# Attention with a local window and a three-way max MLP: the second transpose of each head takes 64 or 96 keys instead of 128

## The chip, the cores and the metric

The kernel runs on one core of a Trainium2 chip. The metric is the device time of one launch in microseconds; a lower time is better. The median of three runs of the kernel before is 864.78 us (864.51 to 865.18).

## The reference

Eight batches of eight heads. Each head has 512 local and 32 global positions of 64 numbers. A local query sees the 32 global keys and the local keys at most 32 positions away; a global query sees all 544 keys. The 8 x 544 = 4352 rows of 512 numbers then go through the MLP.

```python
s_g = scale * np.matmul(q_g, k_all.transpose(0, 1, 3, 2))
out_g = np.matmul(sm(s_g), v_all)
...
mask = np.abs(pos[:, None] - pos[None, :]) <= window      # window = 32
s_ll = np.where(mask, s_ll, -1000000000.0)
s_l = np.concatenate([s_lg, s_ll], axis=-1)
out_l = np.matmul(sm(s_l), np.concatenate([v_g, v_l], axis=2))
...
h = np.maximum(np.maximum(x @ w1, x @ w2), x @ w3)
return h @ w_out
```

## The kernel before, in words

**Tiles of attention.** A pair of heads p has four tiles t of 128 local queries; there are 8 x 4 pairs and so 128 tiles `sl = 4 p + t`, each for both heads j of its pair. `WIN` gives the window of keys of each t, global keys included: 192 keys for t = 0 and 3, and 224 for t = 1 and 2. Each tile passes these steps:

- `scores` (L296): q times k for each head into a bank S. VectorE adds the mask and finds the extreme (L324), ScalarE takes the exponential (L326), and the row is divided by its sum (L329 to L331). The result lies with a query in each partition and the window's keys along the row. For the first 16 tiles (`EARLY`) it stays in `early`, an F32 buffer of four places with rows of 256. For the other 112 a DMA (L333) writes it into one of two buffers `prob` with rows of 256 (type F32R).
- `trans` (L337): turns the probabilities so that keys lie in partitions. The row of 256 is two blocks c of 128 keys. For each head j and block c, a transpose on TensorE (L345) takes the block as its stationary operand and an identity of 128 columns as the moving one (`one` for the early tiles, `identr` for the others), and writes 128 x 128 numbers into a quarter of the bank T. The pool `psT` holds one such bank (`bufs=1`). A copy, and from tile 20 on a subtraction for the low part, takes all 512 columns of T to `pt`.
- `transg` (L356): the same for the global queries' rows, `probg`, into a bank S (L363).
- `pv` (L373): v times the turned probabilities into the bank O. The first 20 tiles use 64 rows of output for each head (L383); the others 128 rows (L391). The rows of v that stand against the keys 192 to 255, or 224 to 255, of a block are zeros.

Since all 256 columns of a row are turned but only 192 or 224 are written, the rest of `early` and `prob` is set to zero once: `early` by L120, and `prob`, with `probg` and `qgz`, by `clear` (L130). Both run on GpSimd (POOL).

**The MLP.** `layer1` (L412) and `layer2` (L438) are generators that issue one matmul at a time (L423, L444). The main loop (L547) is a hand-written order: for each tile it calls the attention steps of the current tile and the ones ahead, and `fill(n)` takes n matmuls of the MLP of the batch before in between, so that TensorE has work while the other engines do softmax. Inside a tile the order is: `trans` of the next tile, 4 MLP matmuls, scores of a later tile, 4, `pv`, global scores, 3, `transg`, 7 (somewhat more in the first 32 tiles). At the end `late` does four pairs' remaining global rows with outputs of 64 rows (L269, L499) and transposes at L489, and the global rows pass the MLP last.

**Order and balance.** `least` deals copies and subtractions to VectorE, ScalarE and GpSimd by a running account of their loads. The framework orders the instructions of the first tiles by its own rules; further on the order of the calls stands.

Of the kernel before, what the change touches and what calls it, by code (L numbers as in the profile page):

```python
# [9 lines left out]
F32 = mybir.dt.float32  # L10
# [20 lines left out]
WIN = [(0, 192), (96, 224), (256, 224), (384, 192)]  # L31
# [19 lines left out]
def f32(ap):  # L51
    return ap.bitcast(F32)


def body(ctx, tc, kin, qin, vin, min_, win, out):
    nc = tc.nc
    act, dve, pool, pe = nc.scalar, nc.vector, nc.gpsimd, nc.tensor
# [7 lines left out]
    psT = ctx.enter_context(tc.tile_pool(name="psT", bufs=1, space=PSUM))  # L65
# [26 lines left out]
    def sub(out, a, b, psum=False):  # L92
        n = width(out)
        c = {"d": n * 1.04 + (160 if psum else 110)}
        if not psum:
            c["p"] = n * 2.32 + 130
        (dve if least(c) == "d" else pool).tensor_tensor(out=out, in0=a, in1=b, op=ALU.subtract)  # L97

    def copy(out, a, psum=False):
        n = width(out)  # L100
        c = {"d": n * (1.04 if psum else 0.52) + (160 if psum else 150), "a": n * 0.833 + (150 if psum else 190)}
        if least(c) == "d":
            dve.tensor_copy(out=out, in_=a)
        else:
            act.copy(out=out, in_=a)  # L105
# [11 lines left out]
    one = const.tile([128, 128], F32, name="one")  # L117
    make_identity(nc, one)
    early = const.tile([128, 4, 2, 256], F32, name="early")
    pool.memset(early[:, :, :, 192:256], 0.0)  # L120
    identr = const.tile([128, 128], F32R, name="identr")
    dve.tensor_copy(out=identr, in_=one)
    mask = const.tile([128, 2, 224], F32, name="mask")
# [2 lines left out]
    prob = [const.tile([128, 2, 256], F32R, name=f"prob{i}") for i in range(2)]  # L126
    probg = [const.tile([128, 3, 128], F32R, name=f"probg{i}") for i in range(2)]
    qgz = const.tile([128, 2, 160], F32R, name="qgz")

    def clear():  # L130
        for t in (*prob, *probg, qgz):
            pool.memset(f32(t), 0.0)

    raw, wt = {}, {}
# [2 lines left out]
        return wt[n][:, 512 * a:512 * a + 512]  # L137

    xg = const.tile([128, NP, B, SG], F32, name="xg")

    spare = [moe.tile([128, 2, 512], I32, name="spare", tag=f"h{f}") for f in (4, 5)]
    loaded, marks = [0], {}
# [194 lines left out]
    def trans(sl):  # L337
        if sl >= NS:
            return
        s = sc.pop(sl)  # L340
        ps = psT.tile([128, 512], F32, name="T")
        pr, ident = (ps, one) if sl < EARLY else (ps.bitcast(F32R), identr)
        for j in range(2):
            for c in range(2):
                pe.transpose(pr[:, 256 * j + 128 * c:256 * j + 128 * c + 128], s[:, j, 128 * c:128 * c + 128], ident)  # L345
        src = ps.rearrange("p (x q) -> p x q", q=128)
        if sl < NAT:
            pt = pts[sl] = att.tile([128, 2, 2, 160], F32, name="pt", tag="pt")
            copy(pt.rearrange("p j c q -> p (j c) q")[:, :, 0:128], src, True)
        else:  # L350
            pt = pts[sl] = att.tile([128, 2, 2, 2, 160], F32R, name="pt", tag="pt")
            v = pt.rearrange("p j c a q -> p (j c) a q")
            copy(v[:, :, 0, 0:128], src, True)
            sub(v[:, :, 1, 0:128], src, f32(v)[:, :, 0, 0:128], True)
# [189 lines left out]
    load_v(SEQ[3], 3)  # L544
    load_weight()
    trans(SEQ[0])
    for i, sl in enumerate(SEQ):  # L547
        p, t = divmod(sl, 4)
        b = p // NP
        settle(4500)  # L550
        if i % 16 == 0 and b > 1:
            fill(400)
            mm[0] = moe_local(b - 1)
        trans(tile_at(i + 1))
        first = i < 32
        fill(6 if first else 4)
        next_scores(i + 3)
        if i < 16:
            if i == 7:
                clear()  # L560
            if i in (10, 12):
                load_k((i - 2) // 2)
            if i == 14:
                split_k(5)
                load_k(6)
        elif t == 3:
            split_k(p + 2)
            load_k(p + 3)
# [95 lines left out]
```

## Time and profile before

| | |
|---|---|
| median of the runs | 864.78 us (864.51 to 865.18) |
| the profiled execution | 865.03 us |
| its span, first to last instruction | 862.9 us |
| mean granted TensorE clock | 0.984 |
| busy: PE, PEld, DVE, ACT, POOL | 820.8, 692.3, 632.0, 505.9, 528.8 us |

PE is TensorE's matmuls and transposes and PEld its weight loads, which run beside them; DVE is VectorE, ACT ScalarE, POOL GpSimd and SP the queue that issues DMAs. A row of a group reads: line, engine, operation, output<-inputs, the part of the array (rows*columns), sizes, count | busy us, mean ns of one | idle time of the engine before them and who ended it. A row of the timeline reads: start in us, length in us, engine, line, operation, output<-inputs, array part, sizes, count of instructions merged. The recorded ends of matmuls are modelled, and matmuls overlap, so a matmul's step is read from one start to the next and not from its length.

### The profile page before, as it was taken

The numbers are of one execution on the slowest core, as the hardware profiler recorded it, in microseconds if no ns is written. First come the engines' busy times: TensorE is split into PE (matmuls) and PEld (weight loads), VectorE is DVE, ScalarE is ACT, GpSimd is POOL, SyncE is SP. The second block draws the span as 40 slices with busy tenths as digits, with TensorE's granted clock in tenths as the row PEclk, the third lists the DMA queues.
The fourth block names the chain that finished last, engine by engine and source line by source line (L and its number), as shares of the span: only waits on it lengthen the run. The fifth ranks groups of instructions, "written<-read, shape, count | busy, mean of one in ns | idle before, by whom it ended". The sixth has DMA issues, their size and how long they took to land.

```text
span 862.9 us, 16816 instructions
## 1 busy us (share of the span) xinstructions
PE 820.8 (95%) x4736; PEld 692.3 (80%) x4736; DVE 632.0 (73%) x2181; ACT 505.9 (59%) x1430; POOL 528.8 (61%) x698
## 2 busy tenths in 40 slices
PE   6878788999999999999999999999999999999997
PEld 5566678988888888888888888888888888777796
DVE  6999798977788888878787888778887876322111
ACT  5666566766676666666666666676666666212111
POOL 5778887866677667756776667667676656111211
PEclk9999688999999999999999999999999999999999
DMA  9743533353334333443325333433344333221000
GB/s 317 261 162 119 160 120 106 111 160 104 111 106 133 120 94 105 130 132 94 101 90 160 106 111 106 136 114 93 109 133 134 94 90 99 77 72 29 28 25 25
DMA packets 99580, 98.72 MB, mean 114 GB/s; under 512 B 21152, under 2 KB 87968, under 8 KB 99488
## 3 DMA queue, kind: packets, MB, share of 16 engines
q1 hardware_dynamic: 99344, 97.43, 36.4%
q8 instruction: 38, 0.62, 0.3%
q14 instruction: 54, 0.44, 0.2%
q10 hardware_dynamic: 144, 0.23, 0.1%
HBM read 60.39 MB, written 8.91 MB: 80 GB/s over the span
## 4 chain that ended last, share of the span: by engine, by line
PE 80%; DVE 8%; POOL 4%; issue 2%; DMA 2%; ACT 2%; SPq 1%; POOLq 0%; DVEq 0%; ACTq 0%
PE pm L423 46%; PE pm L444 15%; PE O L391 6%; PE S L321 5%; PE T L345 4%; PE S L273 1%; POOL h L97 1%; DMA raw<-w_in 1%; POOL w L97 1%; DVE spare L164 1%; DVE spare L160 1%; POOL early L115 1%; PE S L363 1%; DVE s L324 1%; POOL xs L97 1%
## 5 line engine op out<-in xcount | busy, mean ns | idle before, releaser
L423 PE MATMUL pm<-xs,w 128*128 128x512 f32 (+1 forms) x2160 | 504.3, 372 | 5.8 <-POOL w L97 4.5
L423 PEld LDWEIGHTS pm<-xs,w 128*128 128x128 f32 x2160 | 351.9, 193 | 56.4 <-POOL w L97 5.1
L444 PE MATMUL pm<-w,h 128*128 128x512 f32 x612 | 160.4, 399 | 1.7 <-POOL h L97 1.7
L97 POOL TENSOR_TENSOR qs<-qraw,qs 128x256 fp32r<-128x256 f32 x108 | 83.3, 771 | 79.2 <-issue 44.9
L97 POOL TENSOR_TENSOR h<-m,h 128x512 fp32r<-128x512 f32 (+1 forms) x60 | 72.0, 1199 | 88.8 <-ACT h L105 88.8
L444 PEld LDWEIGHTS pm<-w,h 128*128 128x128 f32 x612 | 107.2, 188 | 22.3 <-POOL h L97 3.4
L115 POOL TENSOR_SCALAR s<-s,z 128x224 f32<-128x224 f32 (+1 forms) x212 | 97.0, 466 | 42.3 <-ACT lox L105 19.2
L326 ACT ACTIVATE s<-s,nm 128x192 f32<-128x192 f32 (+1 forms) x224 | 103.3, 462 | 25.0 <-DVE nm L324 16.5
L432 DVE TENSOR_TENSOR m<-pm,m 128x512 f32<-128x512 f32 (+1 forms) x120 | 72.9, 607 | 49.2 <-PE pm L423 47.7
L97 DVE TENSOR_TENSOR pt<-T,pt 128x512 fp32r<-128x512 f32 x108 | 74.5, 690 | 40.7 <-ACT pt L105 38.4
L324 DVE CUSTOM_DVE_ANT_0 s<-S,mask 128x192 f32<-128x192 f32 (+1 forms) x224 | 74.8, 370 | 14.2 <-PE S L321 7.5
L97 POOL TENSOR_TENSOR vs<-vraw,vs 128x256 fp32r<-128x256 f32 x107 | 80.8, 755 | 5.3 <-ACT vs L105 4.1
L105 ACT CAST pt<-T 128x512 fp32r<-128x512 f32 x89 | 52.2, 586 | 48.6 <-PE T L345 48.5
L391 PE MATMUL O<-pt,vs 128*128 128x320 f32 (+1 forms) x432 | 78.3, 303 | 0.1
L391 PEld LDWEIGHTS O<-pt,vs 128*128 128x128 f32 x432 | 70.6, 190 | 9.1 <-DVE pt L97 0.3
L97 POOL TENSOR_TENSOR kst<-kraw,kst 64x576 fp32r<-64x576 f32 x48 | 70.4, 1467 | 5.4 <-DVE nm L324 1.7
L321 PEld LDWEIGHTS S<-kst,qs 128*128 128x128 f32 x432 | 64.9, 194 | 9.7 <-DVE nmg L277 1.8
L105 ACT CAST qs<-qraw 128x256 fp32r<-128x256 f32 x90 | 36.6, 406 | 58.9 <-PE S L321 37.6
L399 DVE TENSOR_TENSOR xr<-O,lox 64x160 f32<-64x160 f32 x216 | 67.9, 314 | 2.8
L345 PEld LDWEIGHTS T<-identr,prob 128*128 128x128 f32 x448 | 50.7, 142 | 19.9 <-ACT s L326 4.7
L321 PE MATMUL S<-kst,qs 128*128 128x192 f32 (+1 forms) x432 | 66.2, 275 | 0.1
L397 DVE TENSOR_TENSOR lox<-O,lox 64x320 f32<-64x320 f32 x108 | 51.6, 478 | 13.5 <-ACT lox L105 7.2
(115 smaller groups left out, 1139.2 us busy)
## 6 DMA issues: line engine op xcount, KB each, us to landing
vraw<-v_in SPq DMA_DIRECT2D x132, 128.0 KB, 2.3
qraw<-q_in SPq DMA_DIRECT2D x108, 128.0 KB, 2.2
prob<-s SPq DMA_DIRECT2D x56, 224.0 KB, 2.4
raw<-w_in SPq DMA_DIRECT2D x24, 512.0 KB, 4.8
prob<-s SPq DMA_DIRECT2D x56, 192.0 KB, 2.3
kraw<-k_in SPq DMA_DIRECT2D x27, 320.0 KB, 3.1
out_dram<-o SPq DMA_DIRECT2D x32, 256.0 KB, 2.3
qn<-q_in SPq DMA_DIRECT2D x21, 128.0 KB, 3.5
```

Of the source, the lines that this page charges most:

```text
L97: (dve if least(c) == "d" else pool).tensor_tensor(out=out, in0=a, in1=b, op=ALU.subtract)
L105: act.copy(out=out, in_=a)
L115: pool.tensor_scalar(out=out, in0=a, scalar1=col, scalar2=1.0, op0=ALU.mult, op1=ALU.mult)
L321: pe.matmul(ph[j][:, 0:n], lhsT=qs[sl][:, a, 128 * j:128 * j + 128], rhs=kst[p][:, j, c0:c0 + n], start=(a == 0), stop=(a == 1))
L324: dve.tensor_tensor_reduce(out=s[:, j, 0:n], in0=ph[j][:, 0:n], in1=mask[:, (1, 0, 1, 0)[t], 32 * (t == 0):32 * (t == 0) + n], scale=-0.12 ...
L326: act.activation(out=s[:, j, 0:n], in_=s[:, j, 0:n], func=AF.Exp, bias=nm[:, j:j + 1], scale=-1.0, accum_out=z[:, j:j + 1])
L345: pe.transpose(pr[:, 256 * j + 128 * c:256 * j + 128 * c + 128], s[:, j, 128 * c:128 * c + 128], ident)
L391: pe.matmul(o[:, j, 0:320].rearrange("p (a q) -> p a q", a=2)[:, :, 0:n], lhsT=vs[sl][:, 2 * j + c].rearrange("p a d -> p (a d)"), rhs=pt[ ...
L399: dve.tensor_tensor(out=xr[p][64 * j:64 * j + 64, t], in0=o[0:64, j, 0:160], in1=lo[:, j], op=ALU.add)
L423: pe.matmul(ps[:, 0:n], lhsT=weight(3 * f + i, w)[:, 128 * k:128 * k + 128], rhs=xs[k][:, a, c0:c0 + n], start=(q == 0), stop=(q == 11))
L432: dve.tensor_tensor(out=m[:, 0:n], in0=ps[:, 0:n], in1=m[:, 0:n], op=ALU.max)
L444: pe.matmul(ps, lhsT=hh[f][:, a, 128 * t:128 * t + 128], rhs=weight(18 + f, w), start=(q == 0), stop=(q == 17))
```

## The change

The second transpose of each head takes only the window's valid keys as its stationary block: `n = WIN[sl % 4][1] - 128`, so 64 keys for t = 0 and 3 and 96 for t = 1 and 2. It writes n rows of its quarter of T. T is no longer taken from its pool for each tile: it is one fixed bank, `turned`, which VectorE sets to zero once at the start, so that the rows that are not written hold finite numbers when the copy takes all 512 columns. The clears of `early` and of the two `prob` go; those of `probg` and `qgz` stay.

```diff
     early = const.tile([128, 4, 2, 256], F32, name="early")
-    pool.memset(early[:, :, :, 192:256], 0.0)
...
     def clear():
-        for t in (*prob, *probg, qgz):
+        for t in (*probg, qgz):
             pool.memset(f32(t), 0.0)
...
+    turned = psT.tile([128, 512], F32, name="T")
+    dve.memset(turned, 0.0)
...
         s = sc.pop(sl)
-        ps = psT.tile([128, 512], F32, name="T")
+        ps, n = turned, WIN[sl % 4][1] - 128
         pr, ident = (ps, one) if sl < EARLY else (ps.bitcast(F32R), identr)
         for j in range(2):
-            for c in range(2):
-                pe.transpose(pr[:, 256 * j + 128 * c:256 * j + 128 * c + 128], s[:, j, 128 * c:128 * c + 128], ident)
+            pe.transpose(pr[:, 256 * j:256 * j + 128], s[:, j, 0:128], ident)
+            pe.transpose(pr[0:n, 256 * j + 128:256 * j + 256], s[:, j, 128:128 + n], ident)
```

PE's order around the transposes of a tile with a window of 192 keys, in the stretch where the MLP's matmuls stand between the steps; `pm` is the MLP's bank, and the sizes are the output's rows x columns. Before:

```order
L363 MATMUL S<-identr,probg_96 128x128
L423 MATMUL pm<-xs,w_400 128x512 x7
L345 MATMUL T<-identr,prob_95 128x128 x4
L423 MATMUL pm<-xs,w_442 128x512 x4
L321 MATMUL S<-kst,qs 128x224 x4
```

After:

```order
L364 MATMUL S<-identr,probg_95 128x128
L424 MATMUL pm<-xs,w_395 128x512 x7
L345 MATMUL T<-identr,prob_94 128x128
L346 MATMUL T<-identr,prob_94 64x128
L345 MATMUL T<-identr,prob_94 128x128
L346 MATMUL T<-identr,prob_94 64x128
L424 MATMUL pm<-xs,w_436 128x512 x4
L322 MATMUL S<-kst,qs 128x224 x4
```

The four transposes stand in the same place. The first and third are as before; the second and fourth have outputs of 64 rows, and in tiles with a window of 224 keys outputs of 96.

POOL's order at the start of the program, where it makes the identity (`masks.py`), clears buffers and divides the first tiles' rows (L115). Before:

```order
masks.py:197 MEMSET one 128x128
L120 MEMSET early 128x8x64
masks.py:199 ISA
masks.py:199 AFFINE_SELECT one<-one 128x128
L132 MEMSET prob_94 128x512
L115 TENSOR_SCALAR early<-early,z 128x224
L132 MEMSET prob_95 128x512
L115 TENSOR_SCALAR early<-early,z 128x224
L132 MEMSET probg_96 128x384
L132 MEMSET probg_97 128x384
L132 MEMSET qgz 128x320
L115 TENSOR_SCALAR early<-early,z 128x192 x2
```

After:

```order
masks.py:197 MEMSET one 128x128
L131 MEMSET probg_95 128x384
masks.py:199 ISA
masks.py:199 AFFINE_SELECT one<-one 128x128
L131 MEMSET probg_96 128x384
L115 TENSOR_SCALAR early<-early,z 128x224 x2
L131 MEMSET qgz 128x320
L115 TENSOR_SCALAR early<-early,z 128x192 x2
```

Three clears are gone, and the clears of `probg` have moved to the places of two of them.

## The prediction

> **What bounds the kernel now.** I read the page first, then the table of stages, then PE's waits, and last the timeline of PE around the edited instructions.
>
> ```profile
> PE 820.8 (95%) x4736; PEld 692.3 (80%) x4736; DVE 632.0 (73%) x2181; ACT 505.9 (59%) x1430; POOL 528.8 (61%) x698
> PE 80%; DVE 8%; POOL 4%; issue 2%; DMA 2%; ACT 2%; SPq 1%; POOLq 0%; DVEq 0%; ACTq 0%
> ```
>
> PE is busy for 95% of the span and makes up 80% of the chain that ended last. The profiled execution took 865.03 us, 862.9 of them span; the median of the runs is 864.78, so 0.25 comes off at the end. Shares are averages, so the table of stages is next (stretch, length, PE busy, PEld, DVE, ACT, POOL, granted clock, DMA share, GB/s):
>
> ```profile
> 80.00:110.00 30.00, 21.56 (x140) 19.24 (x139) 25.05 (x73) 16.38 (x45) 25.74 (x26) 0.77 0.47 147
> 110.00:300.00 190.00, 182.22 (x1088) 159.27 (x1087) 160.39 (x563) 127.93 (x370) 135.13 (x184) 0.96 0.39 118
> 300.00:500.00 200.00, 199.31 (x1101) 168.20 (x1100) 164.11 (x581) 133.47 (x382) 136.36 (x186) 1.00 0.37 112
> 500.00:735.00 235.00, 234.00 (x1291) 197.49 (x1290) 184.34 (x670) 154.30 (x438) 155.04 (x213) 1.00 0.37 111
> ```
>
> From 110 to 735 us PE has hardly a hole, while DVE, the next, has 16 to 22% free. Who PE waits for in that stretch (total, times, longest):
>
> ```profile
> PE S L363 <- DMA probg<-sg: 5.1, 2, 3.0
> PE pm L444 <- POOL h L97: 1.7, 4, 0.7
> PE S L363 <- DVE nm L324: 1.5, 1, 1.5
> PE T L345 <- DMA prob<-s: 0.7, 1, 0.7
> PE T L345 <- DVE z L330: 0.2, 1, 0.2
> ```
>
> That is 9.2 us in 625. So what the edit adds to or takes from PE's own time there reaches the end almost whole. Where the edited transposes lie:
>
> ```profile
> L345 PE MATMUL T<-identr,prob 128*128 128x128 f32 x448 | 52.5, 241 | 5.8 <-DMA prob<-s 5.5 <-DVE z L330 0.2
> L345 PEld LDWEIGHTS T<-identr,prob 128*128 128x128 f32 x448 | 50.7, 142 | 19.9 <-ACT s L326 4.7 <-ACT xr L105 0.8 <-issue 0.7
> L345 PE MATMUL T<-one,early 128*128 128x128 f32 x64 | 12.9, 291 | 12.0 <-POOL early L115 11.5 <-ACT early L113 0.3
> L383 PEld LDWEIGHTS O<-pt,vraw 128*64 128x64 f32 x112 | 7.1, 141 | 3.2 <-issue 1.7 <-ACT pt L105 0.3 <-DMA qn<-q_in 0.2
> ```
>
> ```profile
> L345 PE MATMUL T<-identr,prob x432: 220/245/328, 111.6 to 734.1; 128*128 128x128 f32 x144
> ```
>
> 448 is four for each of 112 tiles; 432 of them, 108 tiles, start between 111.6 and 734.1 us, so inside the full stretch. Windows of 192 keys leave 64 for the second block and those of 224 leave 96; each is every second tile. So **54 tiles with 64-key blocks and 54 with 96-key blocks** lie where PE is the bound.
>
> **The change, part by part: the 64-key blocks.** The pair "128*128" in these rows is the part of the array that an instruction takes. PV of the early tiles (L383) shows that an output of 64 rows runs as "128*64". The program built from the changed kernel says the same of the new transposes: 128x64 for 64 keys, 128x128 for 96. So in each 64-key tile PE goes 128-128, 128-64, 128-128, 128-64 and back: four changes of width where there were none. What that costs is read from starts, since ends are modelled. First, today's group:
>
> ```profile
> 402.03 1.09 PE L423 MATMUL pm<-xs,w 128*128 128x512 f32 x4
> 402.96 0.45 PE L345 MATMUL T<-identr,prob 128*128 128x128 f32 x4
> 403.25 0.70 PE L423 MATMUL pm<-xs,w 128*128 128x512 f32 x2
> ...
> 403.55 0.62 PE L423 MATMUL pm<-xs,w 128*128 128x512 f32 x2
> ```
>
> Four 512-column matmuls take 402.96 − 402.03 = 0.93, so 0.23 each. Four transposes take 0.29, and the matmul behind them 403.55 − 403.25 = 0.30: from the first transpose to the second matmul, 0.59. The ordinary step of one such transpose, alone among wide matmuls, and then the steps with changes of width around them:
>
> ```profile
> 401.22 0.22 PE L363 MATMUL S<-identr,probg 128*128 128x128 f32 x1
> 401.28 1.84 PE L423 MATMUL pm<-xs,w 128*128 128x512 f32 x7
> ```
>
> ```profile
> 769.65 0.40 PE L423 MATMUL pm<-xs,w 128*128 128x512 f32 x1
> 769.97 0.31 PE L499 MATMUL O<-gt,vn 128*64 128x32 f32 x4
> 770.11 0.40 PE L499 MATMUL O<-gt,vraw 128*64 128x32 f32 x6
> 770.44 0.28 PE L489 MATMUL S<-identr,probg 128*128 128x128 f32 x1
> 770.65 0.42 PE L499 MATMUL O<-gt,vraw 128*64 128x32 f32 x6
> ```
>
> ```profile
> 31.51 0.44 PE L345 MATMUL T<-one,early 128*128 128x128 f32 x2
> 31.87 0.43 PE L383 MATMUL O<-pt,vraw 128*64 128x128 f32 x2
> 32.24 0.85 PE L423 MATMUL pm<-xs,w 128*128 128x256 f32 x5
> ```
>
> ```profile
> 747.11 0.74 PE L423 MATMUL pm<-xs,w 128*128 128x512 f32 x2
> ...
> 747.45 0.40 PE L423 MATMUL pm<-xs,w 128*128 128x512 f32 x1
> ```
>
> The ordinary step is 0.06. A 512-column matmul before narrow ones takes 0.32, which is 0.09 over its 0.23: the array empties before the other width may start. The transpose between two narrow groups, 770.44 to 770.65, is the same instruction on the same identity as ours, and takes 0.21: 0.15 over its 0.06, of which 0.09 is again the emptying and 0.06 its own weight load, which nothing covers after a change. The two directions cost alike: a wide pair at 31.51 takes 0.36 and a narrow pair 0.37. And the first 512-column matmul after narrow work takes 0.34 to the next.
>
> So the new group is 0.06 + 0.09 = 0.15 for the first transpose (its load is still ahead of time), 0.21 for each of the other three, and 0.34 for the matmul behind them: 1.12. Net 1.12 − 0.59 = 0.53 us a tile. 54 × 0.53 = **+28.6 us**. This is the term that decides.
>
> The two 64-key tiles of the 112 that come before 111.6 us lie where PE is busy 21.56 of 30 us: between 0 and 2 × 0.53 = 1.1; I take +0.3. Some of the 9.2 us of waits in the full stretch can shrink when PE comes later: between 0 and −2; I take −0.5.
>
> [...]
>
> **The 96-key blocks.** They keep the wide array, so no change of width. Their loads are a quarter shorter at best. Loads cost today's group 0.59 − 4 × 0.06 − 0.23 = 0.12 beyond its streaming, and two of four blocks shrink: between 0 and −0.06 a tile; I take −0.02, since the recorded load is 142 ns for 128 columns and 141 for 64, which shows no gain at all: 54 × −0.02 = **−1.1** (0 to −3.2). That 96 rows cost a change too is a rival below.
>
> **The early tiles.** Eight of 16 have 64 keys. Their PV is narrow already, so the step from the last transpose to PV loses its change of width: 0 to 2 changes more a tile, at 0.15, is 0 to 2.4 us, in a stage where PE waits for others. Against it stand the clears that POOL loses:
>
> ```profile
> L132 POOL MEMSET prob<- 128x512 f32 x2 | 1.1, 526 | 0.0
> ...
> L120 POOL MEMSET early<- 128x512 f32 x1 | 0.5, 529 | 0.0
> ...
> PE T L345 <- POOL early L115: 11.5, 12, 1.6
> ...
> 7.69 0.39 DVE early L324
> ```
>
> They are 1.6 us ahead of POOL's first multiplications, for which PE waits: 0 to −1.6. I put the two together at **0** (−1.6 to +2.4). The new clear of T on DVE stands before DVE's first step of the chain at 7.69, where DVE waits for scores: nothing, or 0.7 (a 128x512 pass) without that cover. The fixed bank adds no wait: T had one buffer before, and its transposes already waited for the copies out of it. Behind its first 80 instructions PE's order is the same; among those some score matmuls trade places, which I price at nothing.
>
> Sum: 28.6 + 0.3 − 0.5 − 1.1 + 0 = 27.3; 865.03 + 27.3 = 892.3, less 0.25: **892 us**. With the small bounds of each term, 886 to 897.
>
> **The rivals.**
>
> *Narrower loads pay (faster).* The mechanism is the load of the block. If a group of transposes in one bank changes width without emptying the array, half of the 0.12 goes in 64-key tiles (0.06) and a quarter in 96-key ones (0.03): 54 × 0.09 = 4.9, so 860. It decides if a change costs under 0.02. For it: loads follow each other closely in the group. Against it: each change of width in these rows, between five kinds of instruction, shows a price. Chance 0.05. [...]
>
> *Half price.* The next load goes out while the array empties, and only the 0.09 is left: 4 × 0.09, less the 0.12 of load delay that is there today, is 0.24 a tile, 13 us: 878. Against it stands the 0.21. Chance 0.07.
>
> *Transposes slow down when narrow.* At the pace of the early ones, (0.36 − 0.15)/2 = 0.105 instead of 0.06, 112 narrow transposes cost 5 more: 897. At four times the 0.06 it is 20 more: 912. No narrow transpose is in this trace. Chance 0.10, the most of it at the lower end. [...] Against the fourfold price, two plain products of 160 columns of the same type took 0.19:
>
> ```profile
> 406.24 0.35 PE L273 MATMUL S<-kst,qgz 128*128 128x160 f32 x2
> 406.43 0.89 PE L423 MATMUL pm<-xs,w 128*128 128x512 f32 x3
> ```
>
> *96 rows change the width too.* Another 54 × 0.53: 920. No 96-row output is in the trace. Chance 0.03.
>
> *Nothing happens.* The chip runs 64 columns as wide; then only the clears are left: 864. Chance 0.02.
>
> **How the numbers follow.** The forecast keeps 0.73. It is 886 to 897; for 8 in 10 I reach up to 902 for the slower narrow transposes and down to 880 towards half price. About 0.2% (1.7 us) is what a measurement of this kernel can tell from none. Faster: the first rival, 0.05, and half of the last, 0.06 in all. Same: 0.01 for the rest of the last, and 0.01 for a price that just cancels, 0.02. Slower: 0.92.
>
> **What would show it.** In the profile after, the narrow transposes should stand as "128*64", 128 of them, and the 96-key ones on the wide array. From the first transpose to the second matmul behind it a 64-key group should take about 1.1 us, a 96-key one 0.55 to 0.6. PE's busy share should stay near 95%, and the span grow between 110 and 765 us alone. I am wrong if the group stays near 0.6, if a 96-key group grows too, or if PE's waits change by more than a few us.

## The result and the profile after

| | before | after |
|---|---|---|
| median, us | 864.78 | 859.88 (859.73 to 860.80, 4 runs) |
| the profiled execution, us | 865.03 | 859.92 |
| its span, us | 862.9 | 858.0 |
| ratio to before | | 0.9945, 95% interval 0.9933 to 0.9957 |

The changed kernel is 4.9 us faster, 0.55%. The forecast was 892, in a range of 880 to 902: the direction was wrong.

The page after, its totals and the chain by engine:

```profile
PE 813.2 (95%) x4736; PEld 683.5 (80%) x4736; DVE 631.0 (74%) x2182; ACT 505.8 (59%) x1430; POOL 526.4 (61%) x695
PE 82%; DVE 5%; DMA 5%; POOL 4%; issue 2%; ACT 1%; SPq 0%; DVEq 0%; POOLq 0%; ACTq 0%
```

PE bounds the kernel as before, with 7.6 us less of busy time. The stages, in the columns of the table in the prediction:

```profile
80.00:110.00 30.00, 20.27 (x133) 17.86 (x133) 25.50 (x76) 16.83 (x49) 25.85 (x26) 0.83 0.45 144
110.00:300.00 190.00, 180.08 (x1091) 156.45 (x1092) 159.77 (x565) 129.08 (x372) 134.28 (x184) 0.98 0.39 119
300.00:500.00 200.00, 199.27 (x1109) 167.72 (x1108) 165.03 (x582) 133.91 (x384) 137.37 (x189) 1.00 0.37 113
500.00:735.00 235.00, 233.96 (x1297) 197.24 (x1297) 183.52 (x662) 152.81 (x433) 153.23 (x209) 1.00 0.36 110
```

PE is nearly as full as it was, but each stretch from 110 us on holds more instructions (300 to 500 us: 1109 for 1101). The granted clock differs from the kernel before up to 300 us (0.83 for 0.77 and 0.98 for 0.96), so the two traces are compared behind 150 us as well, where it is 1.00 in both. The transposes of the full stretch, weight loads and matmuls (least, median and longest ns; first and last start):

```profile
L345 PEld LDWEIGHTS T<-identr,prob x216: 137/141/182, 110.2 to 728.7; 128*128 128x128 f32 x108
L345 PE MATMUL T<-identr,prob x216: 220/225/329, 110.3 to 728.8; 128*128 128x128 f32 x108
L346 PEld LDWEIGHTS T<-identr,prob x216: 109/118/155, 110.3 to 728.8; 128*64 128x64 f32 x54, 128*96 128x96 f32 x54
L346 PE MATMUL T<-identr,prob x216: 221/225/308, 110.4 to 728.8; 128*64 128x128 f32 x54, 128*96 128x128 f32 x54
```

The same transposes ran from 111.6 to 734.1 us before and run from 110.3 to 728.8 now: 622.5 us have become 618.5. So 4.0 us are gained in the full stretch and 1.3 ahead of it, of which 0.4 goes again behind it (128.8 from the last to the end before, 129.2 now). Behind 150 us, at the same granted clock, the gain is almost the same: from the eleventh later tile to the last transpose it is 734.1 − 150.1 = 584.0 us before and 728.8 − 148.7 = 580.1 now, so the clock is not what made the stretch shorter. The narrow blocks stand as "128*64" and "128*96", and their loads are shorter: a median of 118 ns over both for 141, and by width a median of 110 for 64 columns and 125 for 96.

One 64-key group:

```profile
406.08 0.22 PE L345 MATMUL T<-identr,prob 128*128 128x128 f32 x1
406.14 0.23 PE L346 MATMUL T<-identr,prob 128*64 128x128 f32 x1
406.21 0.22 PE L345 MATMUL T<-identr,prob 128*128 128x128 f32 x1
406.27 0.22 PE L346 MATMUL T<-identr,prob 128*64 128x128 f32 x1
406.33 0.69 PE L424 MATMUL pm<-xs,w 128*128 128x512 f32 x2
...
406.63 0.40 PE L424 MATMUL pm<-xs,w 128*128 128x512 f32 x1
```

The steps are 0.06, 0.07, 0.06 and 0.06, where the forecast had 0.15 and three times 0.21. The weight loads of the same group:

```profile
405.85 0.14 PEld L345 LDWEIGHTS T<-identr,prob 128*128 128x128 f32 x1
406.09 0.11 PEld L346 LDWEIGHTS T<-identr,prob 128*64 128x64 f32 x1
406.15 0.14 PEld L345 LDWEIGHTS T<-identr,prob 128*128 128x128 f32 x1
406.23 0.11 PEld L346 LDWEIGHTS T<-identr,prob 128*64 128x64 f32 x1
406.29 0.53 PEld L424 LDWEIGHTS pm<-xs,w 128*128 128x128 f32 x3
```

The next load starts 0.08 after one of 128 columns (406.15 to 406.23) and 0.06 after one of 64 (406.23 to 406.29), and the transpose or matmul that needs it starts 0.04 behind its load (406.27, 406.33). From the first transpose to the second matmul it is 406.63 − 406.08 = 0.55 us, where the forecast had 1.12 and the kernel before 0.59. For all groups behind 111 us that a 512-column matmul follows, the medians of this length in us, worked out from the starts in the traces, are the measure of the experiments below. In the kernel before and in the one with 128-column products, whose groups are all alike, the median is over both kinds.

| kernel | 64-key groups (49) | 96-key groups (49) |
|---|---|---|
| before | 0.598 | 0.598 |
| after | 0.540 | 0.566 |
| narrow blocks as plain F32R products | 0.563 | 0.616 |
| 128-column blocks as plain F32R products | 0.674 | 0.674 |
| narrow blocks as plain F32 products | 1.418 | 0.838 |
| only 64-key tiles narrow | 0.540 | 0.599 |
| only 96-key tiles narrow | 0.598 | 0.563 |
| both wide blocks first | 0.536 | 0.568 |
| all second blocks 32 columns | 0.528 | 0.528 |

### The profile page after: what moved, and what is told of

It is laid out like the page before. It is cut to its first block, busy times and chain, and to the rows that moved or that the text cites. A ratio compares the mean times of both kernels' runs of the same rounds, so it can differ in the third digit from the quotient of the medians.

```text
span 858.0 us, 16764 instructions
## 1 busy us (share of the span) xinstructions
PE 813.2 (95%) x4736; PEld 683.5 (80%) x4736; DVE 631.0 (74%) x2182; ACT 505.8 (59%) x1430; POOL 526.4 (61%) x695
## 4 chain that ended last, share of the span: by engine, by line
PE 82%; DVE 5%; DMA 5%; POOL 4%; issue 2%; ACT 1%; SPq 0%; DVEq 0%; POOLq 0%; ACTq 0%
PE pm L424 47%; PE pm L445 16%; PE O L392 7%; PE S L322 5%; PE T L345 2%; DMA raw<-w_in 2%; PE T L346 2%; PE S L274 1%; POOL h L97 1%; DMA qn<-q_in 1%; POOL xs L97 1%; PE S L364 1%; POOL w L97 1%; POOL early L115 1%; DMA vraw<-v_in 1%
## 5 line engine op out<-in xcount | busy, mean ns | idle before, releaser
L115 POOL TENSOR_SCALAR s<-s,z 128x224 f32<-128x224 f32 (+1 forms) x212 | 97.0, 467 | 42.8 <-ACT lox L105 18.5
L105 ACT CAST h<-m 128x512 fp32r<-128x512 f32 (+1 forms) x59 | 32.9, 558 | 40.6 <-DVE m L433 40.5
```

What stands on the lines that cost most here:

```text
L115: pool.tensor_scalar(out=out, in0=a, scalar1=col, scalar2=1.0, op0=ALU.mult, op1=ALU.mult)
```

## The experiments

Theory A kept as much of the prediction as the result allows: the price of a change of width is real for plain products (an ordinary matmul with the identity as the moving operand), and a transpose is exempt. Its rivals were B, that the price belongs to type F32, and C, that it came from something else around the steps that the prediction read. For the gain, 'loads' (a block of fewer columns loads faster, and that shortens the group) stood against 'clears and order' (the gain comes from the start, where POOL has less to clear and works in another order).

**Narrow blocks as plain products of type F32R.**

```diff
-            pe.transpose(pr[0:n, 256 * j + 128:256 * j + 256], s[:, j, 128:128 + n], ident)
+            if sl < EARLY:
+                pe.transpose(pr[0:n, 256 * j + 128:256 * j + 256], s[:, j, 128:128 + n], ident)
+            else:
+                pe.matmul(ps[0:n, 256 * j + 128:256 * j + 256], lhsT=s[:, j, 128:128 + n], rhs=ident, start=True, stop=True)
```

> The second block of each head in the 112 later tiles is turned by a plain product with the identity, of the same 64 or 96 columns, in place of a transpose. Theory A, the price of a change of width belongs to plain products of 64 columns and a transpose never divides the array: the 64-key groups now pay four changes, 1.12 us from the first transpose to the second matmul behind the group in place of 0.54, and the 96-key groups pay only the longer load of a plain product, some 0.04 a block: 0.6 to 0.65 us. 54 x 0.58 + 54 x 0.07 = 35 us over the changed kernel, 890 to 897 us. Theory B, the price belongs to narrow products of type F32 alone, and these are F32R: no 64-key group over 0.65 us, 862 to 868 us.

Measured 863.97 us (ratio to before 0.9993, 0.9983 to 1.0004), in the range of theory B. A 64-key group of it:

```profile
410.18 0.22 PE L345 MATMUL T<-identr,prob 128*128 128x128 f32 x1
410.24 0.22 PE L349 MATMUL T<-identr,prob 128*64 128x128 f32 x1
410.30 0.25 PE L345 MATMUL T<-identr,prob 128*128 128x128 f32 x1
410.39 0.24 PE L349 MATMUL T<-identr,prob 128*64 128x128 f32 x1
410.46 0.45 PE L427 MATMUL pm<-xs,w 128*128 128x512 f32 x1
...
410.75 0.40 PE L427 MATMUL pm<-xs,w 128*128 128x512 f32 x1
```

A plain product of 64 columns between wide ones costs 0.06 to 0.09 here. Theory A has fallen: a product need not be a transpose to be spared the price.

**128 columns as plain products**, with the clears of `prob` back and `n = 128` in the later tiles.

> The second block of the 112 later tiles keeps 128 columns and is turned by a plain product; the clears of prob are back. It is the control for the run with narrow plain products: the same kind of instruction, no other width. Theory A and theory B both expect only the longer load of a plain product, 0.05 us for each of two blocks: 0.69 us a group against 0.59 to 0.60 in the kernel before, 108 x 0.09 = 10 us, 870 to 877 us. If it comes near 890, the price in the narrow run is that of plain products between transposes and not that of the width.

872.72 us (1.0095, 1.0077 to 1.0114), and groups of 0.674, both close to what was expected. The load of a plain F32R product of 128 columns is longer here than that of a transpose (a mean of 190 ns for 142), and two of them cost 0.076 a group. Against these groups the narrow plain ones save 0.11 (64 columns) and 0.06 (96), with loads of 134 and 164 ns. The gain by columns is there for plain products too.

**Narrow blocks as plain products of type F32.** As the first, with `lhsT=f32(s)[:, j, 128:128 + n], rhs=one`: the same bits, another type.

> The second block of the 112 later tiles is turned by a plain product of type F32 (the same bits, and the F32 identity), with the same 64 or 96 columns. Theory A has fallen: plain narrow products of type F32R paid nothing. Theory B, the price is that of plain products of type F32 with 64 columns: the 64-key groups pay all four changes and the slower pace of F32, 0.15 + 0.26 + 0.21 + 0.26 + 0.34 = 1.2 us in place of 0.54; the 96-key groups, also F32 but on the whole array, pay only pace and load, 0.7 to 0.8 us in place of 0.57. 54 x 0.68 + 54 x 0.2 = 47 us over the changed kernel, 900 to 910 us. Theory C, the price in the early and late narrow steps came from something else around them (their tiles, their place in the program): the 64-key groups are not longer than the 96-key ones, 0.7 to 0.8 us, and the time is 875 to 885 us.

913.31 us (1.0570, 1.0552 to 1.0588). First a 64-key group, then a 96-key group:

```profile
405.13 0.22 PE L345 MATMUL T<-identr,prob 128*128 128x128 f32 x1
405.29 0.43 PE L349 MATMUL T<-one,prob 128*64 128x128 f32 x2
405.65 0.28 PE L345 MATMUL T<-identr,prob 128*128 128x128 f32 x1
405.86 0.43 PE L349 MATMUL T<-one,prob 128*64 128x128 f32 x2
406.22 0.95 PE L427 MATMUL pm<-xs,w 128*128 128x512 f32 x3
...
406.55 0.62 PE L427 MATMUL pm<-xs,w 128*128 128x512 f32 x2
```

```profile
399.01 0.22 PE L345 MATMUL T<-identr,prob 128*128 128x128 f32 x1
399.06 0.41 PE L349 MATMUL T<-one,prob 128*96 128x128 f32 x2
399.23 0.30 PE L345 MATMUL T<-identr,prob 128*128 128x128 f32 x1
399.37 0.41 PE L349 MATMUL T<-one,prob 128*96 128x128 f32 x2
399.53 0.94 PE L427 MATMUL pm<-xs,w 128*128 128x512 f32 x3
...
399.84 0.39 PE L427 MATMUL pm<-xs,w 128*128 128x512 f32 x1
```

The first transpose now takes 405.29 − 405.13 = 0.15 to 0.16 before 64 columns and 0.05 to 0.06 before 96; the second takes 0.21 and 0.14. Those 0.15 and 0.21 are the very steps of the prediction. Between the two kinds of group of this one run, whose blocks differ in the number of columns alone, lie 1.418 − 0.838 = 0.58 us for four changes. So theory B holds in these runs, in its narrow form: the price comes with plain products of type F32 **and** 64 columns (groups of 1.418); at 96 columns of the same type it is not there (0.838), and at 64 columns of type F32R it is not there (0.563). Theory C falls: the price appears in a place where there was none. The group is 1.42 where 1.2 was expected, and the time lies above the 900 to 910 of theory B. A plain F32 product stands as two instructions (x2 in the rows, and 4960 instructions on PE for 4736), which the expectation seems to have counted once: 0.36 from such a product to the transpose behind it, for 0.26. By the groups the whole should be 54 x 0.88 + 54 x 0.27 = 62 us over the changed kernel; 53 were measured. The other 9 are found in PE's waits, which add up to 30.8 us in this trace and to 40.0 in the changed kernel's, as fits a PE that comes later and so waits less for the others.

Type F32 alone, as a transpose, was in the changed kernel all along, in its early tiles:

```profile
17.50 0.33 PE L345 MATMUL T<-one,early 128*128 128x128 f32 x1
17.66 0.27 PE L346 MATMUL T<-one,early 128*64 128x128 f32 x1
17.77 0.30 PE L345 MATMUL T<-one,early 128*128 128x128 f32 x1
17.91 0.27 PE L346 MATMUL T<-one,early 128*64 128x128 f32 x1
18.11 0.65 PE L384 MATMUL O<-pt,vn 128*64 128x128 f32 x6
```

The narrow F32 transpose at 17.66 goes to a wide one in 0.11, the time that a wide F32 transpose at 14.79 us takes to the next (14.90). The one at 17.91 takes 0.20 to the plain F32 product, although both rows say "128*64", and a transpose of 96 columns at 22.26 us takes the same 0.20 to its plain F32 product (at 22.46): the column that I read as a division of the array names the columns in use, and as far as these steps tell, a narrow transpose counts with the wide instructions.

**The global scores on 128 columns.** The reverse: take the narrow plain F32 products away where the kernel has them.

```diff
-            pe.matmul(ps[0:64, 0:n], lhsT=kraw[p][:, KW:KW + 2 * SG], rhs=kraw[p][:, c0:c0 + n], start=True, stop=True)
-            in1 = zero[0:64].to_broadcast([64, n])
+            pe.matmul(ps[:, 0:n], lhsT=kraw[p][:, KW - 64:KW + 2 * SG], rhs=kraw[p][:, c0:c0 + n], start=True, stop=True)
+            in1 = zero[64:128].to_broadcast([64, n])
...
-        dve.tensor_tensor_reduce(out=s[:, s0:s0 + n], in0=ps[0:64, 0:n], in1=in1, scale=-0.125, scalar=3.0e38,
+        dve.tensor_tensor_reduce(out=s[:, s0:s0 + n], in0=ps[64:128, 0:n] if 4 * p in NATK else ps[0:64, 0:n], in1=in1, scale=-0.125, scalar=3.0e38,
```

> The changed kernel with the F32 products of the global scores (two for each of ten steps) on 128 columns of k in place of 64: the 64 columns before the wanted ones are added, and the wanted rows lie in the upper half of the bank. Theory B: without a narrow F32 product there is no change of the array; the 512-column matmul before the late ones takes 0.23 in place of 0.32, the last of them 0.14 in place of 0.23 and the matmul behind them 0.23 to 0.30 in place of 0.34; four late groups, 0.2 to 0.35 us each, 0.8 to 1.4 us: 858.5 to 859.1 us. Rival, the price is that of going to F32 and back at any width: the steps stay 0.32 and 0.23, and the time 859.9.

First the changed kernel at one late step, then this run at the same:

```profile
739.99 0.84 PE L424 MATMUL pm<-xs,w 128*128 128x512 f32 x3
740.76 1.13 PE L270 MATMUL S<-kn 128*64 128x384 f32 x4
741.82 0.98 PE L424 MATMUL pm<-xs,w 128*128 128x512 f32 x3
```

```profile
742.00 0.84 PE L424 MATMUL pm<-xs,w 128*128 128x512 f32 x3
742.68 1.08 PE L270 MATMUL S<-kn 128*128 128x384 f32 x4
743.49 1.21 PE L424 MATMUL pm<-xs,w 128*128 128x512 f32 x4
```

Three matmuls ahead take 0.68 in place of 0.77 and the four rows of the global scores 0.81 in place of 1.06: 0.34 a step, the upper end of the expectation, and the same in all four. So the wide F32 products of this run hold up neither the matmul ahead of them nor their own end, and that part of the price is gone with the 64 columns. The matmul behind still takes 0.34, by the starts, as it does behind the narrow products; the expectation had it fall to between 0.23 and 0.30. So that step does not hang on the 64 columns. And the whole took 859.37 us (0.9950, 0.9938 to 0.9962), not to be told from the changed kernel. PE's waits between 735 and 812 us, in the changed kernel and then in this run (total, times, longest), say where the 4 x 0.34 = 1.4 us went:

```profile
PE S L490 <- issue: 0.8, 2, 0.5
PE S L490 <- DMA probg<-sg: 0.3, 1, 0.3
```

```profile
PE S L490 <- issue: 1.6, 2, 0.9
PE S L490 <- DMA probg<-sg: 0.5, 2, 0.3
```

The waits ahead of the transposes of the global probabilities grow from 1.1 to 2.1 us: 1.0 of the 1.4 comes back.

**The clears back.**

```diff
+    pool.memset(early[:, :, :, 192:256], 0.0)
...
-        for t in (*probg, qgz):
+        for t in (*prob, *probg, qgz):
```

> The changed kernel with the clears of early and prob back on POOL; the blocks stay narrow and the bank fixed. Theory 'loads': the gain comes from the shorter loads, 54 x 0.055 + 54 x 0.03 = 4.6 us at the most, of which 3.9 lie after 110 us; the clears are the 1.1 us that the traces differ by at 40 us: 861.0 us, 1.1 over the changed kernel. Theory 'clears and order': most of the gain is the start: 863 or more.

859.92 us (0.9952, 0.9940 to 0.9965): the time of the changed kernel. Its interval excludes the 863 or more of 'clears and order' and not the 861.0 of 'loads'. What the clears and the order that goes with them give to the end can't be told from nothing. In this trace the fifth later tile's transposes start at 112.4 us, 2.1 later than in the changed kernel's, but the eleventh's at 149.3, only 0.6 later (148.7): what the start costs is made up in the loosely filled stage up to 150 us.

**Only one kind of tile narrow**, with the clears: `n = 64 if WIN[sl % 4][1] == 192 else 128`, and `n = 96 if WIN[sl % 4][1] == 224 else 128`.

> Clears back, and only the 64-key tiles are narrow; the 96-key tiles turn 128 columns as before. Theory 'loads', in which a group is bound by its chain of weight loads and a load's time goes with its columns: 64-key groups 0.54 to 0.55 us, the others 0.59 to 0.60; 54 x 0.054 = 2.9 us under the kernel before, 861.9 us. Theory 'any narrowing breaks the chain once', without regard to the columns: 64-key groups as in the changed kernel, and 2.2 us under before, 862.6 us. Theory A says that no 64-key group is longer than 0.6 us.

> Clears back, and only the 96-key tiles are narrow; the 64-key tiles turn 128 columns as before. Theory 'loads': 96-key groups 0.566 us and the others 0.598; 54 x 0.032 = 1.7 us under the kernel before, 863.0 us, and together with the run of the 64-key tiles alone the whole gain of the change. Rival, 96 columns gain nothing and the change's gain is that of the 64-key tiles: no difference from before.

861.54 us (0.9969, 0.9957 to 0.9981) and 861.87 us (0.9974, 0.9966 to 0.9983). The groups are as 'loads' has them, each kind by itself, and the two gains, 0.31% and 0.26%, add up to 0.57%, against the change's 0.55%. The 96-key tiles gave more at the end (2.2 us, 1.5 to 2.9) than their groups (54 x 0.035 = 1.9), within the interval.

**The second block cut to 32 columns.** `n = WIN[sl % 4][1] - 128 if sl < EARLY else 32`. This kernel leaves the keys beyond 160 of each window out of the output, and stands for its time alone.

> The second block of the 112 later tiles is cut to 32 columns, so that the keys beyond 160 of a window are left out of the output: a run for the time alone. Theory 'loads, down to the floor of streaming': at 64 columns the steps inside the group are 0.060 to 0.062, which is what a transpose alone takes, so a shorter load has nothing left to give: both kinds of group at 0.540, 54 x 0.026 = 1.4 us under the changed kernel, 858.5 us. Rival, the time of a group goes on falling with the columns, 0.0009 us for each: 64-key groups 0.51 and 96-key groups 0.51, 4.6 us under the changed kernel, 855.3 us. If a block of 32 columns paid a change of the array, the groups would be over 1 us.

857.87 us (0.9923, 0.9908 to 0.9938), which is not clear of the changed kernel but excludes the rival's 855.3. Groups of 0.528 lie between the floor of 0.540 and the 0.51 of the rival, nearer to the floor: at 64 columns the steps inside the group have come down to 0.059 to 0.063, a transpose's own pace (0.06 at 401.22 us in the kernel before), and what still falls is the step of the matmul behind (0.294 to 0.282). So 0.540 was not quite the floor.

**Both wide blocks first.** Two loops over j, one for the first blocks and one for the second.

> The changed kernel with the order of the four transposes changed: both first blocks, then both second blocks; the same work. Theory 'loads' (each weight load starts when the transpose ahead of it starts to stream; 0.060 us for 128 columns, less for fewer): the load of the second wide block goes ahead under the step of 0.23 before the group, and the matmul behind the group gets its load earlier. 64-key groups 0.005 to 0.016 us shorter, 96-key groups 0.008: 0.7 to 1.3 us in all, 858.6 to 859.2 us. Rival, the order doesn't matter since the sum of the loads is the same: groups and time as in the changed kernel, 859.9.

858.54 us (0.9934, 0.9921 to 0.9947) is the time that 'loads' gave, but not by its reason: the 64-key groups are 0.004 shorter and the 96-key groups 0.002 longer, as the rival has it. The interval overlaps the changed kernel's, so a gain is not shown. With the edit of the global scores as well:

> The changed kernel with both of these edits, the order of wide blocks first and the global scores on 128 columns. If 'loads' and theory B hold, their gains add: 1.5 to 2.7 us, 857.2 to 858.4 us. If neither holds, 859.9.

858.31 us (0.9933, 0.9921 to 0.9945): inside the range expected, and again not clear of the changed kernel.

## Why the prediction was wrong

*What bounds the kernel.* Right. PE is full from 150 us on, and a change of its own time there reaches the end: groups shorter by 54 x 0.058 + 54 x 0.032 = 4.9 us gave 4.0 in the stretch and 4.9 in the whole. That the 4.9 agree is in part chance, since 1.3 of the whole came ahead of the stretch, at another granted clock. Behind 150 us the 102 groups should give 4.6; PE's waits there grew from 1.9 to 2.7 us, and 3.9 were left.

*The 64-key blocks, +28.6 us: this step failed.* The prediction put it so: an output of 64 rows "runs as 128*64", therefore "four changes of width where there were none". The prices 0.09, 0.15 and 0.21 were read correctly; the steps of 0.15 and 0.21 came back to the hundredth when the block was made a plain F32 product. The 0.34 of the matmul behind came back too, but the wide F32 product has it as well. What was wrong was to whom they belong. Every narrow row that I had (L269, L383, L499) was plain, of type F32 and of 64 columns at once, and I took the one property that the change shares with them for the cause. The instruction with the matching identity and type, L489, stood there as the wide neighbour of a narrow one and told nothing of a narrow transpose. The right sum for this term is 54 x (0.540 − 0.598) = −3.1 us. That the array empties (0.09) and that a load lies uncovered (0.06) were my explanations of the excess; the runs show the steps, and no run shows either.

*The 96-key blocks, −1.1 us.* The sign was right and the size too small: 54 x −0.032 = −1.7 by the groups. I had discounted it because the recorded load was 142 ns for 128 columns and 141 for 64. Those 141 belong to plain F32 products (L383) again. Among transposes a load falls from 141 ns to 125 for 96 columns and 110 for 64. The profile of the kernel before had a sign of it, loads of plain products with 128 columns (type F32R) at 190 ns, to be set beside the 141 of L383:

```profile
L391 PEld LDWEIGHTS O<-pt,vs 128*128 128x128 f32 x432 | 70.6, 190 | 9.1 <-DVE pt L97 0.3
```

*The early tiles and the clears, 0.* Right in effect. For the clears it is shown by the run that has them back; for the narrow early transposes it is read from their steps (0.11 and 0.20, as at 128 and 96 columns), and no run has them apart.

*The rivals.* "Narrower loads pay" happened, with its own numbers: 0.06 and 0.03 a group forecast, 0.058 and 0.032 measured, 860 us forecast and 859.88 measured. It had a chance of 0.05, since I held a price of change to be proven. Against 128 columns, the loads of the transposes are 31 ns shorter at 64 columns and 16 at 96 (110 and 125 for 141), those of the plain F32R products 56 and 26 ns (134 and 164 for 190). What a group can gain is limited by the transposes' own step, 0.060 to 0.062 at 64 columns by the medians: the 0.012 that 32 columns gained came from the matmul behind (0.294 to 0.282). Half price, slower narrow transposes and a price for 96 rows did not occur: the steps of a 64-key group are 0.06 to 0.07, and a 96-key group takes 0.566. The fourfold pace that the prediction weighs for narrow transposes is shown by no run.

*What stays open.* Why the steps around a plain F32 product of 64 columns are longer (0.15 and 0.21) and those around one of type F32R are not (0.06 to 0.09); only the condition is shown. A narrower block also writes fewer rows, and no run has that apart from its shorter load. For the load speaks that the next load starts 0.06 after a narrow one in place of 0.08, at 406.29, when the narrow transpose itself (406.27) has only begun.

## What to carry to other kernels

A price read from a neighbouring instruction is safe for the new one only if kind, type and shape all agree (here one of 0.15 and 0.21 a step came with F32, plain and 64 columns together, and was absent where one of them differed); where the rows at hand differ in three properties at once, each of them is a rival with a real chance. In the short transposes here the columns of the stationary block cost time, those without valid data too, although the moving identity has 128 columns throughout: with second blocks of 128, 96, 64 and 32 columns a group takes 0.598, 0.566, 0.540 and 0.528 us, and from 64 columns down the steps inside it stand at a transpose's own 0.06. Time saved in one step of a stage that waits for a chain of other engines can come back as a wait a few steps on, as 1.0 of 1.4 us did in the late steps.

## What the runs showed of the hardware that was not expected

- Plain F32 products of 64 columns between wide instructions cost 0.58 us for four changes in the F32 run (1.418 for 0.838 at 96 columns) and 0.34 for two in the late steps, so 0.15 to 0.17 a change. F32R products of 64 columns (steps of 0.06 to 0.09), transposes of 64 columns (0.06 for F32R, 0.11 for F32) and F32 products of 96 columns (0.05 to 0.06 for the transpose ahead, 0.15 to 0.16 at 64) or 128 (0.68 for the three matmuls ahead, 0.77 at 64) show no such price.
- "128*64" in a row of the trace gives the columns in use. From one "128*64" row to another the step can still contain the price (0.20 at 17.91 us), and from "128*64" to "128*128" it can be absent (0.07 at 406.14).
- A plain F32 product stands as two instructions in the trace (4960 on PE for 4736, two more for each of 112 tiles); a transpose of the same type stands as one, at 0.11 a step.
- Recorded weight loads of 128, 96 and 64 columns take 142, 127 and 110 ns for transposes and 190, 164 and 134 for plain F32R products (means), so lengths are compared within one kind.
